# Masks added on VectorE from the fourth batch on, and a planner that knows that VectorE and GpSimd exclude each other

## The chip, the cores and the metric

One core of a Trainium2 chip runs the kernel. The metric is device time in microseconds (us). PE is TensorE, DVE is VectorE, ACT is ScalarE, POOL is GpSimd and SP is SyncE, whose queue issues nearly all transfers.

## What is computed

Attention over 8 batches, 8 heads, 576 positions and head size 64, followed by a gated two-layer network over all 4608 tokens (512 to 2048 to 512), all in float32:

```
scores = q k^T / 8, per batch and head
mask, heads 0-3 ("local"):   0 <= row - col < 32
mask, heads 4-7 ("strided"): row >= col and row % 32 == col % 32
attn = softmax(scores where the mask holds, else -1e9)
x    = (attn v), heads side by side, 4608 x 512
h    = x w_in ;  g = h * clip(h + 3, 0, 6) / 6 ;  out = g w_out
```

## The kernel before

**Network.** To keep float32 precision each large product is made of three passes over operands split into a high part and a remainder ("hi" and "lo"). Batches 0 to 2 go through the network one at a time (`ffn`, lines 921 to 923 for the first layer, 854 to 856 for the second). The other five, with the 64 rows left over of every batch, go in three pairs (`ffn_pair`), where one level of a Strassen-like scheme makes seven products of eight (lines 1094 to 1096). Before a pair starts, `combine_x` takes differences of its inputs (line 1039) and splits the results in hi (ACT, line 1030) and lo (POOL or DVE, line 1033). `split_g` splits the gated values in the same way (ACT line 887, POOL line 890). During the first batches the weights come in, are rebuilt and split (lines 311 to 337), and `combine_weights` makes the weight sums for the pairs (lines 974 to 995).

**Attention.** It runs between the network's products, two heads at a time, in `kept_pair`: 32 head pairs, of which 16 are local and 16 strided. For one head pair j = 0, 1:

1. PE, `scores`: two PSUM banks get the mask first, as a product of the identity `eye` with the mask (line 597: 96x384 for a local head, 128x144 for a strided one; line 601 masks one 32x32 corner of a local head more), and the small score products are accumulated on it (line 608, 72 of them for a local pair, 128 for a strided one).
2. `keep` copies each bank to the SBUF tile `e` (ACT line 619, or DVE line 621, whichever the planner finds earlier).
3. DVE takes row maxima (631), POOL subtracts them (653), ACT takes exp (656), DVE sums (659), adds 1e-9 from a tile `eps` and inverts (663, 664), POOL multiplies (668).
4. DVE transposes (708, 713), PE multiplies by v (402, 771), ACT or DVE put the result away.

Only steps 1 and 2 lose or gain instructions in this change, besides the added 1e-9 in step 3.

**What sets the order.** Nothing is dispatched when the kernel runs. A planner (`Plan`) gets every operation with the engines that can do it, an assumed duration on each, what it reads and writes and a due time. `emit` then plays the program through once: it takes again and again the engine and operation that can start first, and writes the instructions in that order. Each engine so has a fixed list, in which an instruction at the head that waits holds up all behind it. For some operations `emit` also chooses the engine. The assumed durations decide the order of the lists, never the duration of an instruction.

Of the kernel before, what the change touches and what calls it, by code (L numbers as in the profile page):

```python
# [10 lines left out]
F32 = mybir.dt.float32  # L11
F32R = mybir.dt.float32r
BF16 = mybir.dt.bfloat16
# [7 lines left out]
P = 128  # L21
# [18 lines left out]
HIENG = {"ACT": 0.63, "POOL": 1.2}  # L40
# [5 lines left out]
SOLO = 3  # L46
PAIRS = ((3, 4), (5, 6), (7, "l"))
# [15 lines left out]
PATIENCE = 2.0  # L63


class Plan:
# [12 lines left out]
    def op(self, engine, us, fn, reads=(), writes=(), due=0.0, room=0.0, mode="", after=0.0, take=None, give=None, early=0.0, words=6):  # L79
# [13 lines left out]
        self.ops.append((how, fn, before, due, room, mode, after, take, give, early, words))  # L93
        return n

    def emit(self, idle):
# [10 lines left out]
        mode, dma = "", 0.0  # L107
# [11 lines left out]
        while done < len(ops):  # L119
            done += 1  # L120
            best = None
            for e, r in ready.items():
                t0, first, kept = free[e], None, 0.0
                for due, n in sorted(r):
                    t = max(t0, avail[n] + (PATIENCE if e == "DVE" and avail[n] > WARM and len(ops[n][0]) > 1 else 0.0))
# [9 lines left out]
                if first is not None and (best is None or first[0] < best[0]):  # L135
                    best = (first[0], e, first[2])
            t, e, n = best
            how, fn, _, due, _, m, after, take, give, _, words = ops[n]
# [48 lines left out]
def attention_ffn(ctx: ExitStack, tc, q, k, v, w_in, w_out, out):  # L187
# [34 lines left out]
    eps = const.tile([P, 2, 8], F32, name="eps")  # L222
# [4 lines left out]
    mtri = const.tile([P, NPOS], BF16, name="mtri")  # L227
    left = [const.tile([P, B * LEFT], F32, name=f"left{c}") for c in range(NCC)]

    def identity():  # L230
        nc.vector.memset(three, 3.0)
        nc.vector.memset(eps, 1.0e-9)
# [30 lines left out]
    op("POOL", 2.2, masks, reads=[("ident",)], writes=["const"], due=-22)  # L263

# [25 lines left out]
    def weight_part(k, w, g, i):  # L290
# [52 lines left out]
        op("DVE", 0.95, join, reads=[key], writes=[fkey], due=due - 3)  # L343
        op(HIENG, 0, hi, reads=[fkey], writes=[key], due=due - 2)
        op({"POOL": 1.4, "DVE": 0.75}, 0, lo, reads=[fkey, key], writes=[key + ("lo",), key], due=due - 1)
# [94 lines left out]
    def kept_pair(g):  # L440
# [150 lines left out]
        sb = [slot(early) for _ in range(2)]  # L591

        def scores():
            ps = [psum(sb[j], f"ps{nm}{j}")[:n, :cols].rearrange("p (u x) -> p u x", x=w) for j in range(2)]
            m = (mband if loc else mtri).unsqueeze(1).to_broadcast([n, nblk, w])
            for j in range(2):
                nc.tensor.matmul(ps[j], eye[:n, :n], m, start=True, stop=False)
            if loc:
# [3 lines left out]
            for i in range(nblk):  # L602
                for a in range(n // PAD):
                    for j in range(2):
# [4 lines left out]
                                         qk_of("k")[own, k0:k0 + w], start=False, stop=i == nblk - 1)  # L609
# [4 lines left out]
        def keep(e, j):  # L614
# [3 lines left out]
            if e == "ACT":  # L618
# [669 lines left out]
```

## Time and profile before

| | us |
|---|---|
| median of three runs (lowest to highest) | 929.01 (928.42 to 932.99) |
| the profiled execution | 929.12 |
| its span, from first to last instruction | 927.3 |
| PE busy | 885.3 (95%) |
| DVE busy | 488.8 (53%) |
| POOL busy | 428.6 (46%) |
| ACT busy | 404.6 (44%) |

The execution that was profiled took 929.12 us, 1.8 us more than its span. In the rows of a timeline the first number is the start in us from the start of the span, the second the duration, and in brackets stands how long the engine was idle ahead of it and what ended that. In rows of a group the last two numbers before the second bar are the busy time in us and the mean duration of one in ns. Matmul instructions overlap in a pipeline: a product of 512 columns is shown as 0.39 us long, but the next one starts 0.23 us after it, and it is the distance of the starts that tells what a product costs.

### The profile page before, as it was taken

To read this page: it belongs to the slowest core of one execution; us is meant where nothing else is said; L and a number is where in the kernel's file an instruction comes from. 1 tells how busy PE (TensorE), PEld (TensorE's weight loads), DVE (VectorE), ACT (ScalarE), POOL (GpSimd) and SP (SyncE) were. 2 spreads that over 40 slices of the span, in tenths; PEclk is the share of its full clock that TensorE was granted. 3 is DMA by queue.
4 is the path that set the end of the run, shared out by engine and by line. 5 is a ranking of instruction groups with operands and counts; after the bars stand their busy time and mean duration, and the time that the engine had idled before them with its cause. 6 is when DMAs were issued, how large, how long until landed. Compare 5 with 4: busy or idle time off the path is not lost.

```text
span 927.3 us, 19470 instructions
## 1 busy us (share of the span) xinstructions
PE 885.3 (95%) x7747; PEld 711.9 (77%) x7747; DVE 488.8 (53%) x833; ACT 404.6 (44%) x736; POOL 428.6 (46%) x378
## 2 busy tenths in 40 slices
PE   5789898999999999999999999999999999999997
PEld 3668686776888788888788778888887887888786
DVE  3788866568766777466755723345457003323200
ACT  2656655333434435344444633444446234334421
POOL 3646765555765877222221955213139531112441
PEclk7579999999999999999999999999999999999999
DMA  9988999977688874799784687785745675555374
GB/s 161 236 251 206 249 236 333 282 177 190 181 197 242 209 189 112 205 260 230 218 209 149 194 257 196 238 210 192 227 156 211 200 236 185 194 192 188 120 213 137
DMA packets 229563, 191.71 MB, mean 207 GB/s; under 512 B 174944, under 2 KB 189280, under 8 KB 229472
## 3 DMA queue, kind: packets, MB, share of 16 engines
q1 hardware_dynamic: 226800, 189.35, 73.2%
q10 hardware_dynamic: 2672, 1.11, 0.6%
q8 instruction: 61, 1.00, 0.5%
q14 instruction: 30, 0.25, 0.1%
HBM read 157.91 MB, written 32.51 MB: 205 GB/s over the span
## 4 chain that ended last, share of the span: by engine, by line
PE 75%; POOL 6%; DMA 6%; DVE 5%; SPq 3%; issue 2%; ACT 2%; DVEq 0%; POOLq 0%; ACTq 0%
PE ph L1094 8%; PE ph L1095 7%; PE ph L1096 7%; PE acc L854 4%; PE acc L856 4%; PE acc L855 4%; PE ph L921 3%; PE ph L922 3%; PE ph L923 3%; PE ps L608 3%; DMA rawi<-in_moe_w_in_dram 3%; DMA qn<-in_q_dram 2%; POOL xc L1033 2%; PE acc2b L854 2%; PE acc2b L856 2%
## 5 line engine op out<-in xcount | busy, mean ns | idle before, releaser
L1113 DVE TENSOR_TENSOR htmp<-ph,htmp 128x512 f32<-128x512 f32 x72 | 49.7, 690 | 183.9 <-ACT htmp L1105 106.7
L1094 PE MATMUL ph<-xc,wi 128*128 128x512 f32 x336 | 133.4, 397 | 1.3 <-DVE htmp L1113 0.8
L1095 PE MATMUL ph<-xc,wi 128*128 128x512 f32 x336 | 131.1, 390 | 0.0
L1096 PE MATMUL ph<-xc,wi 128*128 128x512 f32 x336 | 130.9, 390 | 0.0
L890 POOL TENSOR_TENSOR g<-u,g 128x512 fp32r<-128x512 f32 x48 | 65.7, 1372 | 62.1 <-ACT g L887 50.1
L921 PE MATMUL ph<-x,wi 128*128 128x512 f32 x192 | 79.8, 415 | 7.9 <-DVE u L960 4.6
L922 PE MATMUL ph<-x,wi 128*128 128x512 f32 x192 | 76.8, 400 | 4.0 <-DVE x L433 2.6
L923 PE MATMUL ph<-x,wi 128*128 128x512 f32 x192 | 76.7, 399 | 0.8 <-POOL wi L337 0.8
L854 PE MATMUL acc<-wo,g 128*128 128x512 f32 x192 | 76.9, 401 | 0.0
L855 PE MATMUL acc<-wo,g 128*128 128x512 f32 x192 | 75.1, 391 | 1.5 <-issue 1.1
L1094 PEld LDWEIGHTS ph<-xc,wi 128*128 128x128 f32 x336 | 63.0, 188 | 17.2 <-DVE htmp L1113 2.0
L856 PE MATMUL acc<-wo,g 128*128 128x512 f32 x192 | 75.4, 392 | 0.2 <-POOL g L890 0.2
L1096 PEld LDWEIGHTS ph<-xc,wi 128*128 128x128 f32 x336 | 63.1, 188 | 13.4
L1095 PEld LDWEIGHTS ph<-xc,wi 128*128 128x128 f32 x336 | 63.1, 188 | 12.4
L708 DVE STREAM_TRANSPOSE atloc<-e 32x192 f32<-32x192 f32 x168 | 61.9, 369 | 15.9 <-POOL e L668 9.0
L1105 ACT COPY htmp<-ph 128x512 f32<-128x512 f32 x72 | 42.2, 587 | 50.0 <-PE ph L1096 48.1
L653 POOL TENSOR_TENSOR e<-e,st 128x288 f32<-128x288 f32 (+1 forms) x30 | 34.2, 1141 | 64.5 <-DVE st L631 64.4
L890 POOL TENSOR_TENSOR g12a<-u,g02a 128x512 fp32r<-128x512 f32 x16 | 20.6, 1289 | 83.4 <-ACT g02a L887 83.4
L956 ACT ACTIVATE u<-htmp,three 128x512 f32<-128x512 f32 x48 | 34.7, 723 | 44.5 <-DVE htmp L1113 44.5
L956 ACT ACTIVATE u<-ph,three 128x512 f32<-128x512 f32 x48 | 33.0, 688 | 44.2 <-PE ph L923 43.8
L960 DVE SCALAR_TENSOR_TENSOR u<-u,htmp 128x512 f32<-128x512 f32 x48 | 38.5, 802 | 22.9 <-ACT u L956 22.8
L890 POOL TENSOR_TENSOR g11a<-u,g01a 128x512 fp32r<-128x512 f32 x16 | 21.5, 1347 | 60.4 <-ACT g01a L887 52.2
(212 smaller groups left out, 2079.5 us busy)
## 6 DMA issues: line engine op xcount, KB each, us to landing
wo<-wod SPq DMA_DIRECT2D x128, 512.0 KB
wi<-wid SPq DMA_DIRECT2D x84, 512.0 KB
rawi<-in_moe_w_in_dram SPq DMA_DIRECT2D x16, 512.0 KB
rawo<-in_moe_w_out_dram SPq DMA_DIRECT2D x16, 512.0 KB
wod<-wo SPq DMA_DIRECT2D x16, 512.0 KB
wid<-st SPq DMA_DIRECT2D x64, 128.0 KB
qn<-in_q_dram SPq DMA_DIRECT2D x112, 72.0 KB
kn<-in_k_dram SPq DMA_DIRECT2D x112, 72.0 KB
```

Of the source, the lines that this page charges most:

```text
L708: nc.vector.transpose(at[PAD * (a + h):PAD * (a + h) + PAD, :, PAD * a:PAD * a + PAD], e[PAD * a:PAD * a + PAD, :, PAD * h:PAD * h + PAD])
L854: nc.tensor.matmul(acc, gh, woh, start=fc == 0, stop=False)
L855: nc.tensor.matmul(acc, gh, wol, start=False, stop=False)
L856: nc.tensor.matmul(acc, gl, woh, start=False, stop=end)
L890: on(e).tensor_tensor(out=to(1), in0=tiles[uk], in1=tiles[gk[0]].bitcast(F32), op=ALU.subtract)
L921: nc.tensor.matmul(ph, wih, xh, start=n_ == 0, stop=False)
L922: nc.tensor.matmul(ph, wih, xl, start=False, stop=False)
L923: nc.tensor.matmul(ph, wil, xh, start=False, stop=n_ == NCC - 1)
L956: nc.scalar.activation(make(), src(), AF.Relu, bias=three)
L1094: nc.tensor.matmul(ph, w[:, j, 0], x[:, 0], start=u in (0, 1, 3) and j == 0, stop=False, skip_group_check=u in (2, 4, 5, 6))
L1095: nc.tensor.matmul(ph, w[:, j, 0], x[:, 1], start=False, stop=False, skip_group_check=u in (2, 4, 5, 6))
L1096: nc.tensor.matmul(ph, w[:, j, 1], x[:, 0], start=False, stop=j == 1, skip_group_check=u in (2, 4, 5, 6))
```

## The change

It has two parts.

**The masks.** From batch 3 on (`ADDED = 3`), so for 20 of the 32 head pairs, the products of lines 597 and 601 are left out; each small score product now starts and ends its own piece of the bank (`start=added`). `keep` is then DVE's alone: one addition of the bank and a mask, 96x384 with the new tile `mwhole` for a local head, 128x144 with `mtri` for a strided one. POOL fills `mwhole` once (a copy of six masks and a memset).

**The planner.** An operation can be marked `port`. Marked ones on DVE and POOL are planned so that none overlaps another on the other engine. Marked are the operations of POOL in attention, the splits, sums and differences of weights and inputs, POOL's `split_g`, and a gate on DVE whose second input lies in SBUF. Some assumed durations are changed with it (POOL's high part of a weight from 1.2 to 0.62 us), the delay that kept DVE from taking shared work early is 0 for marked operations, and ties between engines are broken by due time. The 1e-9 is now added as a constant, so `eps` is gone.

Parts left out of the diff only mark further operations with `port=True` and change assumed durations by a few hundredths.

```
-HIENG = {"ACT": 0.63, "POOL": 1.2}
+HIENG = {"ACT": 0.63, "POOL": 0.62}
...
+ADDED = 3
...
-PATIENCE = 2.0
+PATIENCE = {("DVE", False): 2.0, ("DVE", True): 0.0, ("POOL", True): 0.0}
+PORT = ("DVE", "POOL")
...
-                    t = max(t0, avail[n] + (PATIENCE if e == "DVE" and avail[n] > WARM and len(ops[n][0]) > 1 else 0.0))
+                    t = max(t0, avail[n] + (PATIENCE.get((e, ops[n][11]), 0.0) if avail[n] > WARM and len(ops[n][0]) > 1 else 0.0))
+                    if ops[n][11] and e in PORT:
+                        t = max(t, port)
...
-                if first is not None and (best is None or first[0] < best[0]):
-                    best = (first[0], e, first[2])
+                if first is not None and (best is None or first[:2] < best[3]):
+                    best = (first[0], e, first[2], first[:2])
...
             free[e] = end = t + (us() if callable(us) else us)
+            if shared and e in PORT:
+                port = end - 0.13
...
+    def whole_mask():
+        nc.gpsimd.tensor_copy(mwhole, mband.unsqueeze(1).to_broadcast([QB, NQB, 2 * PAD]))
+        nc.gpsimd.memset(mwhole[:PAD, 0, :PAD], NEG)
+    op("POOL", 0.9, whole_mask, reads=["const"], writes=["mwhole"], due=T0 + TILE + 20, early=T0 + TILE)
...
-        op({"POOL": 1.4, "DVE": 0.75}, 0, lo, reads=[fkey, key], writes=[key + ("lo",), key], due=due - 1)
+        op({"POOL": 1.29, "DVE": 0.68}, 0, lo, reads=[fkey, key], writes=[key + ("lo",), key], due=due - 1, port=True)
...
+        added = b >= ADDED
...
-            for j in range(2):
+            for j in range(0 if added else 2):
                 nc.tensor.matmul(ps[j], eye[:n, :n], m, start=True, stop=False)
-            if loc:
+            if loc and not added:
...
-                                         qk_of("k")[own, k0:k0 + w], start=False, stop=i == nblk - 1)
+                                         qk_of("k")[own, k0:k0 + w], start=added, stop=added or i == nblk - 1)
...
-            if e == "ACT":
+            if added:
+                nc.vector.tensor_tensor(out=e_own(j), in0=ps, in1=mwhole if loc else mtri.unsqueeze(1).to_broadcast([n, nblk, w]), op=ALU.add)
+            elif e == "ACT":
                 nc.scalar.copy(e_own(j), in_halves(ps))
...
-            nc.vector.tensor_tensor(out=x, in0=x, in1=eps[:n, :, :nblk], op=ALU.add)
+            nc.vector.tensor_scalar_add(x, x, 1.0e-9)
...
-                op({"POOL": 0.74, "DVE": 0.42}, 0, mix, reads=w, writes=[w[to[0]]], due=due + kc + 0.1)
+                op({"POOL": 0.74, "DVE": 0.42}, 0, mix, reads=w, writes=[w[to[0]]], due=due + kc + 0.1, port=True)
```

**How the lists move.** Line numbers of the changed kernel are 10 to 13 higher behind the inserted lines: 608 becomes 619, 890 becomes 903, 1033 becomes 1046, 1039 becomes 1052. The first place is PE's list at the scores of a local head pair of the first pair of batches; `ps_10` and `ps_11` are its two banks. Before:

```order
L856 MATMUL acc0a_5177<-wo_5604,g10a_5880 128x512
L597 LDWEIGHTS eye
L597 MATMUL ps_10_5970<-mband,eye 96x384
L597 MATMUL ps_11_5971<-mband,eye 96x384
L601 LDWEIGHTS eye
L601 MATMUL ps_10_5970<-mfirst,eye 32x32
L601 MATMUL ps_11_5971<-mfirst,eye 32x32
L608 MATMUL ps_10_5970<-kplain,qplain 32x64
L608 MATMUL ps_11_5971<-kplain,qplain 32x64
```

After:

```order
L867 MATMUL acc0a_5170<-wo_5584,g00a_5823 128x512
L868 MATMUL acc0a_5170<-wo_5584,g00a_5823 128x512
L869 MATMUL acc0a_5170<-wo_5584,g10a_5832 128x512
L619 MATMUL ps_10_5957<-kplain,qplain 32x64
L619 MATMUL ps_11_5958<-kplain,qplain 32x64
```

The four mask products and their weight loads are gone; the network's product stands directly ahead of the first score product.

The second place is POOL's list where the second pair of batches is got ready (`combine_x`) while the first pair's products still run; `g10a` is the lo part of a gated value, which PE waits for, `xc` and `hxf` are the inputs that are split and subtracted. Before:

```order
L1033 TENSOR_TENSOR xc_3_6487<-hxf_2009,xc_3_6487 128x512
L890 TENSOR_TENSOR g10a_6520<-u_14_6460,g00a_6500 128x512
L1033 TENSOR_TENSOR xc_3_6512<-hxf_2062,xc_3_6512 128x512
L1033 TENSOR_TENSOR xc_6_6528<-hxf_2089,xc_6_6528 128x512
L1033 TENSOR_TENSOR xc_6_6545<-hxf_2099,xc_6_6545 128x512
L1039 TENSOR_TENSOR hxf_2089<-hxf_2089,hxf_2009 128x512
L1039 TENSOR_TENSOR hxf_2099<-hxf_2099,hxf_2062 128x512
L890 TENSOR_TENSOR g10a_6590<-u_15_6561,g00a_6573 128x512
L890 TENSOR_TENSOR g10b_6607<-g_0_5208,g00b_6582 128x512
```

After:

```order
L1052 TENSOR_TENSOR hxf_2055<-hxf_2088,hxf_2055 128x512
L1046 TENSOR_TENSOR xc_1_6404<-hxf_2098,xc_1_6404 128x512
L903 TENSOR_TENSOR g10a_6458<-u_14_6411,g00a_6451 128x512
L1052 TENSOR_TENSOR hxf_2068<-hxf_2098,hxf_2068 128x512
L1046 TENSOR_TENSOR xc_6_6476<-hxf_2088,xc_6_6476 128x512
L1052 TENSOR_TENSOR hxf_2088<-hxf_2088,hxf_2055 128x512
L1046 TENSOR_TENSOR xc_4_6463<-hxf_2068,xc_4_6463 128x512
L1052 TENSOR_TENSOR hxf_2088<-hxf_2088 128x512
L903 TENSOR_TENSOR g10a_6549<-u_15_6510,g00a_6539 128x512
L903 TENSOR_TENSOR g10b_6564<-g_0_5167,g00b_6529 128x512
```

From the first `xc` of this place on, eleven operations of lines 1033 and 1039 and two `g10a` stand ahead of the last `g10a` before, and nine of lines 1046 and 1052 and one `g10a` after. In all POOL has fourteen operations of these two lines at this place before and twelve after; the other two have gone to DVE. Over the whole program POOL's share of line 1033 goes from 27 to 19 and of line 1039 from 15 to 21, DVE's from 15 to 23 and from 9 to 3; of the weights' remainders (line 337) three go from DVE to POOL, and of their high parts (lines 327 and 329) four from ACT to POOL.

The third place is DVE's list at the strided scores that follow the local ones of the first place. Before:

```order
L960 SCALAR_TENSOR_TENSOR u_11_6266<-u_11_6266,htmp_1984 128x512
L631 TENSOR_REDUCE st_3_6273<-e 128x16
L659 TENSOR_REDUCE st_3_6273<-e 128x16
L663 TENSOR_TENSOR st_3_6273<-st_3_6273,eps 128x16
L664 RECIPROCAL st_3_6273<-st_3_6273 128x16
L1113 TENSOR_TENSOR htmp_1984<-ph_6_1_6288,htmp_1984 128x512
```

After:

```order
L1126 TENSOR_TENSOR htmp_1988<-ph_6_1_6166,htmp_1988 128x512
L973 SCALAR_TENSOR_TENSOR u_12_6191<-u_12_6191,htmp_1988 128x512
L630 TENSOR_TENSOR e<-ps_30_6193,mtri 128x8x18
L630 TENSOR_TENSOR e<-ps_31_6194,mtri 128x8x18
L644 TENSOR_REDUCE st_3_6263<-e 128x16
L672 TENSOR_REDUCE st_3_6263<-e 128x16
L676 TENSOR_SCALAR st_3_6263<-st_3_6263 128x16
L677 RECIPROCAL st_3_6263<-st_3_6263 128x16
```

The two evictions are new in DVE's list, directly ahead of the row maxima, which were there before.

More of the change, by code (lines that the diff above doesn't have):

```diff
@@ L77, in __init__, with op @@
         self.by = {}
-    def op(self, engine, us, fn, reads=(), writes=(), due=0.0, room=0.0, mode="", after=0.0, take=None, give=None, early=0.0, words=6):
+    def op(self, engine, us, fn, reads=(), writes=(), due=0.0, room=0.0, mode="", after=0.0, take=None, give=None, early=0.0, words=6, port=False):
         n = len(self.ops)
@@ L92, in op @@
         how = engine if isinstance(engine, dict) else {engine: us}
-        self.ops.append((how, fn, before, due, room, mode, after, take, give, early, words))
+        self.ops.append((how, fn, before, due, room, mode, after, take, give, early, words, port))
         return n
@@ L134, in emit @@
                         first = (t, due, n)
-                if first is not None and (best is None or first[0] < best[0]):
-                    best = (first[0], e, first[2])
-            t, e, n = best
-            how, fn, _, due, _, m, after, take, give, _, words = ops[n]
+                if first is not None and (best is None or first[:2] < best[3]):
+                    best = (first[0], e, first[2], first[:2])
+            t, e, n, _ = best
+            how, fn, _, due, _, m, after, take, give, _, words, shared = ops[n]
             for x in how:
@@ L227, in attention_ffn @@
     mtri = const.tile([P, NPOS], BF16, name="mtri")
+    mwhole = const.tile([QB, NQB, 2 * PAD], BF16, name="mwhole")
     left = [const.tile([P, B * LEFT], F32, name=f"left{c}") for c in range(NCC)]
@@ L678, in kept_pair @@
             op("DVE", red, most, reads=[ekey, ekey + "1"], writes=[stkey], due=sd + 0.7)
-            op("POOL", pool, less, reads=[stkey, ekey + "1"], writes=[ekey], due=sd + 1)
+            op("POOL", pool, less, reads=[stkey, ekey + "1"], writes=[ekey], due=sd + 1, port=True)
             op("ACT", 0.2 + 0.0017 * cols, exp, writes=[ekey], due=sd + 1.5)
@@ L961, in gate_of @@
         op("ACT", 0.69, relu, reads=reads, writes=[uk], due=due)
-        op({"DVE": 0.69, "POOL": 1.4} if both else {"DVE": 0.69}, 0, gate, reads=reads, writes=[uk], give=give, due=due)
+        op({"DVE": 0.69, "POOL": 1.4} if both else {"DVE": 0.69}, 0, gate, reads=reads, writes=[uk], give=give, due=due, port=give is not None)
     def combine_weights(g, due):
@@ L974, in whole @@
                     on(e).tensor_tensor(out=tiles[tk.key].rearrange("p (u x) -> p u x", u=FQ), in0=a, in1=d, op=ALU.add)
-                op({"POOL": 1.34, "DVE": 0.69}, 0, whole, reads=[key, key + ("lo",), "tmps"], writes=[tk], take=tk, due=due + kc, early=due)
+                op({"POOL": 1.3, "DVE": 0.69}, 0, whole, reads=[key, key + ("lo",), "tmps"], writes=[tk], take=tk, due=due + kc, early=due, port=True)
                 w.append(tk)
@@ L1002, in combine_weights @@
                 op("ACT", 0.63, hi, reads=[w[i]], writes=[sk, sk + ("lo",)], due=due + kc + 0.2)
-                op({"POOL": 1.34, "DVE": 0.69}, 0, lo, writes=[sk, w[i]], due=due + kc + 0.3, give=w[i])
+                op({"POOL": 1.3, "DVE": 0.69}, 0, lo, writes=[sk, w[i]], due=due + kc + 0.3, give=w[i], port=True)
                 op("SP", 1.4, put, reads=[sk], writes=[("wid", 7 * (2 * g + f) + u, kc) for f in range(2) for u in us], due=due + 3, after=2.0)
```

24 lines of the change are left out of this document (11 added, 13 removed).

## The prediction

> **What bounds the kernel now.** I read the page's head and its chain first, then the busy time by stretch, then single places of the timeline.
>
> ```profile
> span 927.3 us, 19470 instructions
> PE 885.3 (95%) x7747; PEld 711.9 (77%) x7747; DVE 488.8 (53%) x833; ACT 404.6 (44%) x736; POOL 428.6 (46%) x378
> PE 75%; POOL 6%; DMA 6%; DVE 5%; SPq 3%; issue 2%; ACT 2%; DVEq 0%; POOLq 0%; ACTq 0%
> ...
> 0.00:75.00 75.00, 56.06 (x908) 43.23 (x909) 49.32 (x97) 36.92 (x76) 39.39 (x63) 0.73 0.99 215
> 75.00:222.00 147.00, 136.96 (x1388) 107.74 (x1389) 108.01 (x189) 73.56 (x137) 88.67 (x74) 1.00 0.90 244
> 222.00:500.00 278.00, 277.24 (x3134) 223.20 (x3134) 188.81 (x344) 123.42 (x237) 138.73 (x121) 1.00 0.77 201
> 500.00:545.00 45.00, 42.80 (x212) 34.31 (x212) 26.14 (x26) 24.48 (x44) 32.15 (x22) 1.00 0.70 208
> 545.00:690.00 145.00, 145.00 (x1120) 118.43 (x1119) 60.67 (x109) 56.72 (x98) 41.44 (x34) 1.00 0.70 208
> 690.00:725.00 35.00, 32.70 (x140) 25.80 (x141) 18.59 (x16) 20.40 (x37) 32.47 (x23) 1.00 0.56 199
> ```
>
> The last six rows give, per stretch: its length, then busy us of PE, weight loads, DVE, ACT and POOL (instructions in brackets), the granted clock, the DMA share, GB/s. Up to 75 us PE lacks 18.9 us and the DMA share is 0.99: inputs and weights come in. From 75 to 222 it lacks another 10.0. From 222 to 500 and from 545 to 690 it lacks 0.8 us in 423, at full clock: there every product that goes is time that goes. In the two stretches where the next pair's inputs are got ready (500 to 545, 690 to 725) it lacks 2.2 and 2.3, and POOL is the fullest of the others (32.47 of 35.00). All 20 head pairs that the change touches have their scores between 222 and 679 us (the evictions in line 619's row below start from 224.1 to 678.5), nearly all in the full stretches.
>
> **The masks on PE.** One local and one strided pair, and a place where the network's products are followed at once by small ones with no mask between:
>
> ```profile
> 467.74 0.39 PE L856 MATMUL acc0a<-wo,g10a 128*128 128x512 f32 x1
> 467.97 0.49 PE L597 MATMUL ps<-mband,eye 96*96 96x384 bf16 x2
> 468.39 0.21 PE L601 MATMUL ps<-mfirst,eye 32*32 32x32 bf16 x2
> 468.53 0.97 PE L608 MATMUL ps<-kplain,qplain 64*32 64x64 f32 x72
> ...
> 489.83 0.39 PE L856 MATMUL acc0a<-wo,g10a 128*128 128x512 f32 x1
> 490.06 0.30 PE L597 MATMUL ps<-mtri,eye 128*128 128x144 bf16 x2
> 490.29 1.27 PE L608 MATMUL ps<-kplain,sq 64*32 64x18 f32 x128
> ...
> 485.66 0.39 PE L1096 MATMUL ph<-xc,wi 128*128 128x512 f32 x1
> 485.98 1.28 PE L402 MATMUL pv<-atloc,vloc 128*64 128x96 f32 x28
> ```
>
> By distances of starts: the local masks take 468.53 - 467.97 = 0.56 us, the strided ones 490.29 - 490.06 = 0.23. But the network's product ahead of them costs 0.23 (467.97 - 467.74), and ahead of small products without a mask it costs 0.32 (485.98 - 485.66). That change of kind, 0.09, now falls to it. So a local pair saves 0.56 - 0.09 = 0.47 and a strided one 0.23 - 0.09 = 0.14; ten of each make 4.7 + 1.4 = **6.1 us**. No row shows a network product directly ahead of line 608, so this is bounded: if the change of kind is free there, 5.6 + 2.3 = 7.9; if the first weight load (0.11 us by the row below), which now has no mask to hide under, shows as well, 20 x 0.11 less, 3.9. I take 6.1, since line 402 is the nearest case.
>
> **The evictions on DVE.** Forty copies leave ACT and forty additions come to DVE.
>
> ```profile
> L608 PEld LDWEIGHTS ps<-kplain,qplain 64*32 64x32 f32 x1152 | 13.9, 113 | 0.6
> L1113 DVE TENSOR_TENSOR htmp<-ph,htmp 128x512 f32<-128x512 f32 x72 | 49.7, 690 | 183.9 <-ACT htmp L1105 106.7
> L619 ACT COPY e<-ps x40: 263/381/482, 224.1 to 678.5; 96x384 f32<-96x384 f32 x20, 128x144 f32<-128x144 f32 x20
> L621 DVE COPY e<-ps x4: 307/426/554, 16.1 to 104.6; 96x384 f32<-96x384 f32 x2, 128x144 f32<-128x144 f32 x2
>   ACT e L619: 46.2, 14
> ```
>
> DVE's own copies of these banks took 0.307 us (144 columns) and 0.554 (384); an addition with one input in PSUM took 0.690 for 512 (line 1113), less than 0.554 x 512 / 384 = 0.739. So I price an addition like the copy of its size: 20 x 0.554 + 20 x 0.307 = 17.2 us of DVE; the copies are the lower end, 40 x 0.690 = 27.6 the upper one : 13.8 of the 17.2 for the 16 pairs in 222 to 500, where DVE has 89 us to spare. I cost them at nothing on the path. What hides them: PE has the network's products to go on with, and DVE stood idle 46.2 us (last row: idle time of DVE ahead of its rows on `e` between 222 and 690 that ACT's copy ended, 14 times) in which it waited for just these evictions; now it does them then. Behind an eviction in DVE's list stand the row maxima, which need it anyway, and only then the next gate. Without that cover the price is the 17.2 (a rival below). [...]
>
> **The planner's new order.** The pieces of work are the same but for a few that change engines, so what it can win are stalls of PE. The ones behind POOL and DVE in the two full-POOL stretches:
>
> ```profile
> 529.83 1.72 POOL L890 TENSOR_TENSOR g10a<-u,g00a 128x512 fp32r<-128x512 f32 x1
> 531.61 0.50 PE L856 MATMUL acc0a<-wo,g10a 128*128 128x512 f32 x1 [1.52 <-POOL g10a L890]
> 537.49 0.50 PE L854 MATMUL acc0b<-wo,g00b 128*128 128x512 f32 x1 [0.59 <-ACT htmp L866]
> 706.98 0.50 PE L1094 MATMUL ph<-xc,wi 128*128 128x512 f32 x1 [0.43 <-DVE g L960]
> 710.29 0.50 PE L856 MATMUL acc1a<-wo,g11a 128*128 128x512 f32 x1 [1.21 <-POOL g11a L890]
> 718.04 0.50 PE L856 MATMUL acc1b<-wo,g11b 128*128 128x512 f32 x1 [0.65 <-POOL g11b L890]
> ...
> 519.25 1.30 POOL L1033 TENSOR_TENSOR xc<-hxf,xc 128x512 fp32r<-128x512 f32 x1
> 517.25 0.68 DVE L1039 TENSOR_TENSOR hxf<-hxf 128x512 f32<-128x512 f32 x1
> 533.27 1.78 DVE L1033 TENSOR_TENSOR xc<-hxf,xc 128x512 fp32r<-128x512 f32 x1
> ```
>
> At 531.61 PE waits 1.52 us for the last `g10a`. Ahead of it, counted from the first `xc`, stood 13 operations in POOL's list; now there are 10. Three fewer at 1.30 each are 3.9 us, more than the wait: **1.5 us** saved, at most 2.2 (all that PE lacks in that stretch). Around 710 the `g11a` in question is the fourteenth from the first `xc` both before and after: nothing. A DVE operation with two SBUF inputs takes 0.68 us alone and 1.78 beside POOL, so each operation that POOL gives up adds one to DVE that POOL in turn may have to wait for; with two of them at 0.68 the gain is still 3.9 - 1.4 = 2.5, over 1.52. [...]
>
> Before 222 us the list changes on every engine: `kp` ahead of `qp`, and of the weights three remainders and four high parts come to POOL.
>
> ```profile
> 12.55 1.19 PE L498 MATMUL qp<-ident,qn 72*128 72x72 f32 x8 [2.47 <-DMA qn<-in_q_dram]
> L337 POOL TENSOR_TENSOR wi<-fi,wi 128x512 fp32r<-128x512 f32 x12 | 17.0, 1419 | 0.5 <-ACT wi L327 0.2
> L329 POOL CAST wo<-fo 128x512 fp32r<-128x512 f32 x9 | 6.3, 700 | 12.8 <-DVE fo L319 11.3 <-ACT left L419 1.5
> PE ph L921 <- DVE u L960: 4.6, 4, 2.2
> PE ph L923 <- POOL wi L337: 0.8, 1, 0.8
> PE acc L855 <- POOL wo L337: 0.5, 1, 0.5
> ```
>
> For the better, the four waits for DVE's gate (4.6 us in all) could go, as DVE has less to do there; for the worse, POOL gets 3 x 1.42 + 4 x 0.70 = 7.1 us more, and PE already waits for its remainders at two places (last two rows). If `kn` lands ahead of `qn`, whose landing PE awaited 2.47 us, the first scores start up to that much sooner; its landing isn't shown. I take 0 between -4.6 and +7.1, since SP's list is the same for its first 62 rows and the DMA share of 0.99 sets the pace up to 75 us. The added 1e-9 and the `mwhole` copy are off the path: DVE and POOL have 39 and 58 us free between 75 and 222.
>
> **The sum.** 929.12 - 6.1 - 1.5 = **921.5 us**, made against the profiled execution, which is within 0.11 of the median 929.01. [...]
>
> **Rivals.**
>
> *The start gives it back.* POOL becomes what PE waits for while weights are split, between 75 and 222. For it: POOL gets more there, and PE waited for its remainders already. Against it: the two waits were 1.3 us together, and POOL was busy 88.67 of 147. If all 7.1 us landed on PE: 921.5 + 7.1 = 928.6, no change.
>
> *DVE's list becomes the bound.* An eviction at the head of DVE's list waits for its scores, and gates and sums that release PE's banks wait behind it. For it: DVE was the fullest engine beside PE in 222 to 500 (188.81 of 278), and PE did wait for its gate four times earlier on. Against it: it waited there for nothing of note from 222 to 500. With every eviction on the path: 921.5 + 17.2 = 938.7. It decides from the point where more than 7.6 of the 17.2 show, some 18 of 40 evictions: from there the kernel is slower than before.
>
> *The order wins more.* Half of the 10.0 us that PE lacks between 75 and 222, and the 1.9 of line 890 around 710 go as well: 921.5 - 5.0 - 1.9 = 914.6. For it: the old plan let DVE and POOL run side by side where the trace shows 1.78 for 0.68. Against it: the list around 710 has its `g11a` at the same place.
>
> **Chances.** Forecast 0.60 (its own range 917.5 to 925.0, from the bounds 3.9 and 7.9 of the masks and about 2 of order), start gives it back 0.17, DVE 0.11, more 0.12. A measurement of this kernel can tell about 0.5% from no change, 4.6 us: faster is below 924.4. The forecast lies there for 0.51 of its 0.60, "more" wholly: faster 0.63. The rest of the forecast and 0.16 of the first rival make same 0.25. Slower 0.12 is DVE and what the start could cost beyond 7.1. The range 914.5 to 931.0 leaves out about half of "more" (0.05) and the slower cases (0.12).
>
> **What would show it.** The masks: the first score product 0.32 us behind the network's product ahead of it, and each pair's stage on PE shorter by 0.47 or 0.14. The evictions: 0.31 and 0.55 us each, row maxima no later behind the scores than now, and no new wait of PE for DVE from 222 on. The order: no wait for `g10a` around 525. It would be wrong if PE lacks more than 10 us between 75 and 222, or more than 1 us between 222 and 500.

## The result, and the profile after

The changed kernel takes **922.57 us** (median of 8 runs, 918.54 to 925.55) where the kernel before, on the same chip, takes 929.56 (927.68 to 933.06): ratio **0.9915, 95% interval 0.9889 to 0.9941**. Ratios here are worked out over all undisturbed runs and not from the two medians, and one disturbed run of a kernel below (the masks alone), of 1254.29 us, is left out of its ratio. The changed kernel is faster by more than the 0.5% that can be told from no change, and lies 1.1 us from the forecast. The profiled execution took 918.60 us, so it is one of the shortest; the trace tells where a run of 918.6 us has its time. The page's head, its chain, and the busy time in the same six stretches as shown of before (length, then PE, weight loads, DVE, ACT, POOL, then clock, DMA share, GB/s):

```profile
span 916.8 us, 19372 instructions
PE 880.2 (96%) x7686; PEld 709.1 (77%) x7686; DVE 510.0 (56%) x886; ACT 387.9 (42%) x681; POOL 429.2 (47%) x381
PE 78%; DVE 5%; DMA 3%; SPq 2%; issue 2%; POOL 2%; ACT 1%; DVEq 0%; ACTq 0%; POOLq 0%
...
0.00:75.00 75.00, 57.71 (x918) 44.44 (x919) 51.78 (x104) 39.55 (x77) 45.80 (x70) 0.73 0.93 213
75.00:222.00 147.00, 140.20 (x1460) 110.65 (x1459) 108.50 (x191) 68.83 (x125) 89.16 (x80) 0.98 0.90 247
222.00:500.00 278.00, 273.37 (x3023) 220.27 (x3022) 199.28 (x376) 112.72 (x205) 136.40 (x115) 1.00 0.78 203
500.00:545.00 45.00, 44.27 (x219) 35.65 (x219) 29.98 (x32) 25.52 (x44) 28.96 (x20) 1.00 0.73 225
545.00:690.00 145.00, 144.96 (x1112) 118.54 (x1112) 67.47 (x121) 58.45 (x99) 50.32 (x39) 1.00 0.67 198
690.00:725.00 35.00, 35.00 (x155) 28.53 (x154) 15.73 (x13) 16.20 (x29) 26.95 (x19) 1.00 0.75 259
```

POOL's share of the chain fell from 6% to 2%. PE is busy 5.1 us less in all (885.3 to 880.2). What it lacks by stretch, length less busy time: up to 75 us 18.9 before and 17.3 now; 75 to 222, 10.0 and 6.8; **222 to 500, 0.8 and 4.6**; 500 to 545, 2.2 and 0.7; 690 to 725, 2.3 and 0.0. So the forecast's number was met with one loss in it that was not forecast, and more gain elsewhere.

**A measure that the start blurs less.** Runs of one kernel differ by 3 to 10 us here, and two profiles of the changed kernel show the first network product at 42.25 and 41.27 us, and the end of the first pass over the network at 170.83 and 171.33. I therefore also read the *tail*: from the start of the last product of that first pass (the last `acc` of tile 0) to the start of the last product of all (`acc2b`). Those two rows of the timeline, before:

```profile
172.36 0.39 PE L856 MATMUL acc<-wo,g 128*128 128x512 f32 x1
...
922.24 0.39 PE L856 MATMUL acc2b<-wo,ge 128*128 128x512 f32 x1
```

and of the changed kernel, with one row more between them that is used below:

```profile
170.83 0.39 PE L869 MATMUL acc<-wo,g 128*128 128x512 f32 x1
...
219.16 0.39 PE L869 MATMUL acc<-wo,g 128*128 128x512 f32 x1
...
911.75 0.39 PE L869 MATMUL acc2b<-wo,ge 128*128 128x512 f32 x1
```

The tail fell from 749.9 to 740.9 us, by 9.0. The same kernel profiled again below has 741.2, and a kernel whose order differs from before's only at the start has 749.7 against 749.9.

These pairs agree within 0.3 us, but a tail of one profile isn't always that good. The row at 219.16 is the 264th `acc` product, the last one ahead of batch 3's first scores. Up to it the changed kernel and seven of the kernels below have the same instructions on PE, DVE, ACT and POOL, and from the first row to this one their nine traces take from 47.2 to 51.4 us. The two longest (49.5 and 51.4) hold a stretch in which PE ran at half its clock (granted clock 0.50). Kernels with this start are therefore also compared *behind 220*, from the start of the 264th `acc` product to the start of the last `acc2b`: 692.6 us for the changed kernel, 693.4 when it was profiled again. All 20 pairs whose masks moved lie in both measures. Before's order has less other work ahead of its 264th product, so against it only the tail is used.

### The profile page after: what moved, and what is told of

Its sections match the earlier page's. It is cut to its first block, busy times and chain, and to the rows that moved or that the text cites. A ratio compares the mean times of both kernels' runs of the same rounds, so it can differ in the third digit from the quotient of the medians.

```text
span 916.8 us, 19372 instructions
## 1 busy us (share of the span) xinstructions
PE 880.2 (96%) x7686; PEld 709.1 (77%) x7686; DVE 510.0 (56%) x886; ACT 387.9 (42%) x681; POOL 429.2 (47%) x381
## 4 chain that ended last, share of the span: by engine, by line
PE 78%; DVE 5%; DMA 3%; SPq 2%; issue 2%; POOL 2%; ACT 1%; DVEq 0%; ACTq 0%; POOLq 0%
PE ph L1107 9%; PE ph L1109 8%; PE ph L1108 8%; PE acc L867 4%; PE ph L934 3%; PE acc L868 3%; PE acc L869 3%; PE ph L936 3%; PE ph L935 3%; PE ps L619 3%; PE pv L412 2%; PE acc1a L867 2%; PE acc2b L867 2%; PE acc1b L867 2%; PE acc1a L869 2%
## 5 line engine op out<-in xcount | busy, mean ns | idle before, releaser
L903 POOL TENSOR_TENSOR g<-u,g 128x512 fp32r<-128x512 f32 x48 | 63.5, 1326 | 61.0 <-ACT g L900 41.1
L1109 PEld LDWEIGHTS ph<-xc,wi 128*128 128x128 f32 x336 | 63.1, 188 | 13.8 <-issue 0.5
L1108 PEld LDWEIGHTS ph<-xc,wi 128*128 128x128 f32 x336 | 63.1, 188 | 12.3
L681 POOL TENSOR_TENSOR e<-e,st 128x288 f32<-128x288 f32 (+1 forms) x30 | 35.6, 1186 | 33.9 <-DVE st L677 29.9
L666 POOL TENSOR_TENSOR e<-e,st 128x288 f32<-128x288 f32 (+1 forms) x30 | 34.2, 1140 | 35.6 <-DVE st L644 31.4
L903 POOL TENSOR_TENSOR g10a<-u,g00a 128x512 fp32r<-128x512 f32 x16 | 20.6, 1289 | 64.0 <-ACT g00a L900 52.4
```

The costliest lines, as they stand in the source:

```text
L903: on(e).tensor_tensor(out=to(1), in0=tiles[uk], in1=tiles[gk[0]].bitcast(F32), op=ALU.subtract)
L1108: nc.tensor.matmul(ph, w[:, j, 0], x[:, 1], start=False, stop=False, skip_group_check=u in (2, 4, 5, 6))
L1109: nc.tensor.matmul(ph, w[:, j, 1], x[:, 0], start=False, stop=j == 1, skip_group_check=u in (2, 4, 5, 6))
```

## The experiments

All are compared with the kernel before on the same chip. Four kernels part the change first.

**The order alone.** Every mask stays on TensorE; the planner's new prices, waits and shared port are kept.

```diff
-ADDED = 3
+ADDED = 99
```

> The new order alone: the planner's new prices, waits and shared port as in the changed kernel, every mask still added by TensorE and the scores evicted as before the change. Theory (three parts that add up: masks -6.1 us on TensorE, evictions in VectorE's list +3.5, order -4.4, together the -7.0 that was measured): 925.2 us, with the waits of PE for g10a, g11a and g11b gone. [...] Rival B (the order did it all, the masks only move PE's work): 922.6.

Measured: 922.18 us, ratio 0.9913 (0.9888 to 0.9937): by itself as much as the whole change, as rival B's 922.6 had it, and 3.0 us less than my theory. The tail is 745.4, 4.5 under before. PE lacks 2.5 us in 222 to 500, 0.2 in 500 to 545 and 0.1 in 690 to 725. That the order only moves stalls, and leaves this run at the time of before, is refuted; of the 1.5 us that I gave the order, the trace shows three times as much. On rival B the traces and the runs differ: behind 220 the trace has 697.0 us here, 3.6 to 4.4 more than those of the changed kernel, with a stretch at half clock in it (0.50 from 366.4 to 369.7 us), and it was taken in one of the longer runs (925.42 of 918.56 to 928.00).

**The masks alone.** The planner of before, with its prices; masks of batches 3 and later added by VectorE (the planner orders anew, as it now knows those evictions). Cut, against the kernel before:

```diff
+ADDED = 3
...
+        added = b >= ADDED
...
-            for j in range(2):
+            for j in range(0 if added else 2):
...
-            if e == "ACT":
+            if added:
+                nc.vector.tensor_tensor(out=e_own(j), in0=ps, in1=..., op=ALU.add)
+            elif e == "ACT":
```

> The masks alone: the planner of before with its prices, and from the fourth batch on the masks added by VectorE as it evicts. Theory: -6.1 for the masks and +3.5 for evictions that stand ahead of gates in VectorE's list, 927.0 us, with new waits of PE for DVE's u between 222 and 340. [...] Rival B: 929.6. If instead the new order is what makes the waits for u (not the evictions), it is 923.5 without such waits.

Measured: 929.53 us, ratio 0.9981 (0.9972 to 0.9990), 1.8 us less than before; tail 749.3, 0.6 less. The row of 222 to 500 and its longest waits of PE (total, times, longest):

```profile
222.00:500.00 278.00, 271.55 (x3077) 216.96 (x3076) 204.88 (x372) 111.30 (x204) 142.36 (x121) 1.00 0.77 200
PE ph L1105 <- issue: 1.9, 1, 1.9
PE ps L617 <- DVE x L441: 1.4, 1, 1.4
PE pv L410 <- DVE e L628: 1.3, 1, 1.3
```

PE lacks 6.5 us there where it lacked 0.8: what the masks free, waits of several kinds take back. The expected waits for `u` between 222 and 340 are not among them, so the place that I named was wrong; the last row shown is a wait for an eviction (`e`, line 628).

**Masks on both engines, in the changed kernel's order.** The mask products go back to TensorE beside VectorE's addition (the masks are added twice). **Masks on TensorE, the 40 evictions on ScalarE, in the same order.** The second differs from the first only in who evicts:

```diff
-            for j in range(0 if added else 2):
+            for j in range(2):
...
-            if loc and not added:
+            if loc:
```

and in the second also:

```diff
-            if added:
-                nc.vector.tensor_tensor(out=e_own(j), in0=ps, in1=..., op=ALU.add)
-            elif e == "ACT":
+            if added or e == "ACT":
                 nc.scalar.copy(e_own(j), in_halves(ps))
```

> The changed kernel in its own order, with the mask products put back on TensorE beside VectorE's addition (the masks are added twice). Against the changed kernel this is the price of the mask products alone. Theory: 20 pairs at 0.47 or 0.14 us, +6.1, so 928.7 us (926.5 to 930.5 by the bounds 3.9 and 7.9); the first score product again 0.56 or 0.23 behind the network's product plus its 0.23. [...] Rival B (PE has slack where the masks stood, since it then waits for the gate anyway): less than +2, at most 924.6.

> The changed kernel's own order of everything else, with the masks on TensorE and the same 40 evictions made by ScalarE at the places where VectorE made them. Against the run with the masks added twice this is the price of the 40 evictions on VectorE. Theory (evictions ahead of gates cost 3.5 us between 222 and 340): 928.7 - 3.5 = 925.2 us, and the waits for u there are gone. Rival A (evictions wholly hidden): 928.7, the same as with the masks twice. A third way (ScalarE's list holds them up, as it was idle time of DVE behind ACT's evictions before: 46.2 us): above 930.

Measured: 924.79 us, 0.9931 (0.9913 to 0.9948), tail 745.4; and 925.77, 0.9938 (0.9923 to 0.9952), tail 746.3. So at a fixed order the evictions on VectorE are hardly dearer than those on ScalarE: the ratios agree within their intervals, and behind 220 the traces have 697.5 us with them and 696.8 without. (The tail is 0.9 us shorter with them, but the other trace has a stretch at half clock, 0.50 at 203 to 207 us, ahead of the first moved mask.) Against the changed kernel the mask products alone cost 4.0 to 4.9 us behind 220 and 1.5 to 1.9 by the ratios: less than the theory's 6.1, and by the ratios what rival B had, under 2. My theory that the evictions cost 3.5 us fell here, although 925.77 is near the 925.2 that it gave; by the waits, PE waits for `u` 1.8 to 1.9 us in 222 to 500 in both runs.

The next three leave the masks out altogether, or look at the start.

**Keys first.** Before's planner with the new rule for ties alone.

```diff
-                if first is not None and (best is None or first[0] < best[0]):
+                if first is not None and (best is None or first[:2] < best[3]):
```

> The kernel before with one line of the planner changed: of two operations on different engines that could start at the same time, the one that is due sooner is put down first. The only thing this moves is kp ahead of qp at the start (the two transposes of the first pair, and their copies); everything behind stands as before. Theory S (the new order's gain comes in good part from the start, whose first network product stood 2.9 us earlier with the order alone): 3 us less than before, ratio 0.997. Rival J (it is lost again before the end of the first pass over the network, as that end stood 0.8 us later there in spite of the earlier start, so the gain of the order comes from the joints): within 0.5 us of before, ratio 1.000.

Measured: 929.10 us, ratio 0.9983 (0.9965 to 1.0002); first network product at 44.88 instead of 45.59, tail 749.7. That is 1.6 us by the runs and not told from nothing; the rule is at most a part of what the start gives.

**No masks, in before's order** and **in the changed kernel's order**, both with the evictions on ScalarE. Cut: the corner masks and the start flags follow in both, and in the second ScalarE evicts as above.

```diff
+            left_out = b >= 3
-            for j in range(2):
+            for j in range(0 if left_out else 2):
```

> The kernel before in its own order, with the mask products of the fourth and later batches left out and nothing put in their place (the masks are missing there, the evictions stay on ScalarE). Theory M (the mask products cost PE 6.1 us, and what ate them in the run with the masks alone was the evictions in VectorE's list): 6.1 us less than before, ratio 0.9934. Rival W (a PE that is ahead runs into the gates and sums of the other engines in 222 to 500, whoever evicts): about 1.8 us less, ratio 0.998, and PE lacks about 6 us in 222 to 500 instead of 0.8.

> The changed kernel's order with the 40 evictions on ScalarE and the mask products of the fourth and later batches left out, nothing in their place (the masks are missing there). Against the run with these masks on TensorE and these evictions on ScalarE (ratio 0.9938) it gives the masks' price in the new order: theory M 6.1 us less, ratio 0.987; rival W 2 us less, ratio 0.9915. Against the changed kernel (ratio 0.9915) it gives the price of VectorE's evictions: nothing if they are hidden in the new order (the two runs before this one differed by 0.9 us), 4 us if the evictions take the gain.

Measured in before's order: 923.90 us, ratio 0.9924 (0.9897 to 0.9950), tail 744.8: 5.0 us shorter, where theory M had 6.1. PE stays full:

```profile
222.00:500.00 278.00, 277.12 (x3132) 222.84 (x3120) 189.82 (x346) 125.38 (x241) 139.70 (x121) 1.00 0.78 204
```

Rival W, that a PE which is ahead must wait for the others whoever evicts, is refuted by this row: without the new evictions, in the order that suits the old ones, it lacks 0.9.

In the changed kernel's order: 919.25 us, ratio 0.9878 (0.9852 to 0.9903). The two rows of the tail and the 264th `acc` product between them, with the masks on TensorE (evictions on ScalarE):

```profile
172.03 0.39 PE L867 MATMUL acc<-wo,g 128*128 128x512 f32 x1
...
221.54 0.39 PE L867 MATMUL acc<-wo,g 128*128 128x512 f32 x1
...
918.30 0.39 PE L867 MATMUL acc2b<-wo,ge 128*128 128x512 f32 x1
```

and without them:

```profile
170.08 0.39 PE L868 MATMUL acc<-wo,g 128*128 128x512 f32 x1
...
217.39 0.39 PE L868 MATMUL acc<-wo,g 128*128 128x512 f32 x1
...
911.61 0.39 PE L868 MATMUL acc2b<-wo,ge 128*128 128x512 f32 x1
```

The tails are 746.3 and 741.5, but 2.2 of these 4.8 us lie ahead of the first moved mask. Behind 220, at 696.8 and 694.2, the masks are worth 2.6 us in the traces, and 5.6 by the ratios (0.9938 less 0.9878). The waits of PE in 222 to 500 of the run without masks and without VectorE's evictions:

```profile
PE ph L933 <- DVE u L972: 2.3, 3, 0.9
PE ps L620 <- issue: 1.1, 1, 1.1
```

and of the changed kernel, which has them:

```profile
PE ph L934 <- DVE u L973: 2.3, 3, 0.9
PE ps L619 <- issue: 1.0, 1, 1.0
PE pv L412 <- DVE e L630: 0.9, 1, 0.9
```

The waits for the gate's `u` are the same to a tenth with VectorE's evictions and without. They belong to the order. The last row, 0.9 us for an eviction (`e`, line 630), is not among the waits without them. One of the waits for `u`, with what DVE does meanwhile, in the changed kernel's timelines of PE and of DVE:

```profile
243.93 0.50 PE L934 MATMUL ph<-x,wi 128*128 128x512 f32 x1 [0.74 <-DVE u L973]
...
239.58 3.58 DVE L726 STREAM_TRANSPOSE at<-e 32x256 f32<-32x256 f32 x8
243.19 0.69 DVE L973 SCALAR_TENSOR_TENSOR u<-u,ph 128x512 f32<-128x512 f32 x1
243.79 1.01 DVE L630 TENSOR_TENSOR e<-ps,mwhole 96x384 f32<-96x384 f32 x2
```

The gate stands behind eight transposes of the strided softmax, 3.58 us, and the evictions come after it.

**The changed kernel again.** 

> The changed kernel itself once more, beside the two runs without masks on the same chip. Its runs so far lay between 918.5 and 925.6, those of the order alone between 918.6 and 928.0, so 8 runs each can't tell whether the masks bring 0 or 4 us on top of the order. Theory M with hidden evictions: 4 to 6 us below the order alone, ratio 0.987. Rival W: the same as the order alone, ratio 0.9913.

Measured: 923.46 us, ratio 0.9911 (0.9885 to 0.9937), tail 741.2. By the ratio that is rival W's number (0.9913), not theory M's 0.987. Against the run without masks (tail 741.5, behind 220 694.2) VectorE's evictions cost nothing in the traces (741.2 and 693.4); by the ratios they cost 0.0033, 3 us. The two kernels have the same instructions in the same order up to 219 us, so their starts differ by chance alone. Both profiled runs of the changed kernel (918.60 and 919.35) lie at the low end of its own 14 runs (918.5 to 925.6), so what its other runs lose more is in no trace here, and this difference stays open.

The last four try the limits.

**Each addition made twice.**

```diff
+                for _ in range(2):
                     nc.vector.tensor_tensor(out=e_own(j), in0=ps, in1=..., op=ALU.add)
```

> The changed kernel in its own order, with each of the 40 evictions that add a mask made twice on VectorE, one behind the other, into the same tile (the second only repeats the first): 20 x 0.545 + 20 x 0.299 = 16.9 us more of VectorE. If the evictions are hidden, as the prediction had it and as the traces from the end of the first network pass (about 171 us) on say (741.5 us without them, 740.9 and 741.2 with them): not over 1 us longer from there on, time within 2 us of the changed kernel, ratio 0.991 to 0.993. If they take the 3 to 4 us by which the medians stand apart (919.3 without, 922.6 and 923.5 with): 3 to 4 us more again, ratio 0.995. If wholly on the path: 16.9 more, ratio 1.009.

Measured: 926.29 us, ratio 0.9968 (0.9947 to 0.9989), tail 746.2. Of the second 16.9 us of VectorE 5.2 show in the tail, 5.6 to 6.4 behind 220, and 5 by the ratios. That is nearest to the second case, whose 0.995 lies inside the interval, but in the traces the first 16.9 us cost nothing: there the price of evictions is not one rate, and the cover seems nearly used up by the first.

**No shared port.** The order alone, without the rule that marked operations on DVE and POOL don't overlap.

```diff
-ADDED = 3
+ADDED = 99
...
-PORT = ("DVE", "POOL")
+PORT = ()
```

> The order alone (masks on TensorE, ratio 0.9913), with one rule of the planner taken out: operations that read two SBUF tiles on VectorE and GpSimd may again be planned side by side. The other planner edits stay. Theory: this rule is what took away the waits for g10a, g11a and g11b at the joints, 3.4 us; without it PE lacks 2 us or more again in each of the two joints and the ratio is 0.995. Rival: the high parts given to GpSimd and the smaller patience did it; the joints stay without waits, ratio 0.991. [...]

Measured: 945.30 us, ratio 1.0191 (1.0165 to 1.0218), tail 763.3, 17.9 longer than with the rule. Three stretches:

```profile
222.00:500.00 278.00, 268.05 (x3081) 213.32 (x3064) 195.03 (x347) 116.96 (x228) 125.62 (x101) 1.00 0.74 194
500.00:545.00 45.00, 42.95 (x212) 34.32 (x212) 30.88 (x39) 23.42 (x43) 25.44 (x18) 1.00 0.51 170
690.00:725.00 35.00, 32.07 (x165) 25.43 (x164) 27.17 (x35) 20.06 (x34) 23.14 (x17) 1.00 0.47 166
```

Both joints lack 2 us or more again (2.1 and 2.9), as expected, though PE now waits for ACT's `htmp` at both (2.0 and 1.8 us), for `g11a` (1.2) at the second, and not for `g10a`. The largest part of the loss is in 222 to 500, where PE lacks 10.0 us instead of 2.5, which I hadn't expected. The planner's new prices (0.69 and 1.29 us) are near what such operations took with none of the other engine beside them (before, 0.68 us on DVE at 517.25 and 1.29 on POOL at 518.01); without the rule, as I read it, the planner believes them where they don't hold. In the traces 51 of VectorE's `TENSOR_TENSOR` and `SCALAR_TENSOR_TENSOR` operations take over 1.2 us here, 39 with the rule, 37 before. So the rule brings no fewer such operations than the dearer prices of before did; it seems to make the lower prices usable. That the rule alone would make the gain was not tried.

**From batch 5 on**, and **local pairs only**.

```diff
-ADDED = 3
+ADDED = 5
```

and for the other:

```diff
-        added = b >= ADDED
+        added = b >= ADDED and loc
```

> The changed kernel with the masks moved to VectorE only from the batch numbered 5 on (numbered from 0; the change has 3): the eight head pairs of batches 3 and 4 keep their masks on TensorE, and the planner orders anew. Theory: 8 of the 20 pairs' masks, 2.0 us of TensorE by what the runs gave per pair, come back; if the waits of PE for DVE's gate between 222 and 340 (2.3 us) come from VectorE's evictions they go, and the two cancel: ratio 0.991. If those waits come from the order alone, as the run without VectorE's evictions had them too, they stay where this order has them, and it is 2 us slower: ratio 0.993.

> The changed kernel with only the local pairs' masks moved to VectorE; the ten strided pairs keep masks on TensorE and may be evicted by either engine, and the planner orders anew. Theory (a strided pair saves 0.14 us, a local one 0.47): 1.4 us of TensorE come back, and VectorE has 6 us less to do; within 1.5 us of the changed kernel, ratio 0.991 to 0.9925. Rival (the evictions cost on the path what the medians say, 3 to 4 us for all, so over 1 us for the 20 strided ones): no loss or a gain, ratio 0.990.

Measured: 919.06 us, ratio 0.9891 (0.9873 to 0.9910), tail 743.6; and 920.22, ratio 0.9905 (0.9887 to 0.9923), tail 740.0. From batch 5 on, PE is full again in 222 to 500 (its row below, without waits for `u`), but lacks 1.5 us in 545 to 690:

```profile
222.00:500.00 278.00, 277.40 (x3123) 223.90 (x3123) 201.10 (x367) 118.63 (x222) 138.95 (x115) 1.00 0.80 205
```

Its tail is 2.5 us longer than the changed kernel's, but this lies ahead of the first moved mask, in instructions that both have: from the end of the first pass to the 264th `acc` product it took 51.4 us against 48.3 and 47.7, with half clock from 185.2 to 188.5 us (granted clock 0.50). Behind 220 it has 692.2 us against 692.6 and 693.4, and by the ratios it is 2 us faster. So the eight pairs' masks, put back on TensorE with an order of their own, cost nothing that shows. It was profiled once, in the longest of its runs (921.34 of 916.18 to 921.34). Both versions' intervals overlap the changed kernel's, so neither is shown to beat it. That the ten strided pairs' masks on VectorE are worth anything isn't seen: without them, in an order of its own, the tail is 0.9 us shorter, and the time behind 220, 692.4 us, is 0.2 to 1.0 shorter.

The runs together, with the end of the first pass, the tail, and for kernels of the changed kernel's start the time behind 220, read at the same rows in each trace:

| kernel | ratio to before | first pass ends | tail | behind 220 |
|---|---|---|---|---|
| before | 1 | 172.4 | 749.9 | - |
| masks alone | 0.9981 | 174.3 | 749.3 | - |
| keys first | 0.9983 | 171.2 | 749.7 | - |
| no masks, before's order | 0.9924 | 171.9 | 744.8 | - |
| order alone | 0.9913 | 173.2 | 745.4 | 697.0 |
| masks on TensorE, ScalarE evicts | 0.9938 | 172.0 | 746.3 | 696.8 |
| masks on both | 0.9931 | 172.2 | 745.4 | 697.5 |
| no masks, ScalarE evicts | 0.9878 | 170.1 | 741.5 | 694.2 |
| changed | 0.9915, 0.9911 | 170.8, 171.3 | 740.9, 741.2 | 692.6, 693.4 |
| additions twice | 0.9968 | 173.7 | 746.2 | 699.0 |
| no shared port | 1.0191 | 172.6 | 763.3 | - |
| from batch 5 | 0.9891 | 170.7 | 743.6 | 692.2 |
| local only | 0.9905 | 173.8 | 740.0 | 692.4 |

## Why the prediction was right, and where it was not

One step at a time in the changed kernel's order, the traces give: the order -3.6 us (tail 749.9 to 746.3; -5.8 without the 2.2 us that this trace takes more ahead of the first moved mask), the masks off PE -2.6 (696.8 to 694.2 behind 220), the evictions to VectorE -0.8 to -1.6 (to 693.4 and 692.6). The ratios give -5.8 (0.9938), -5.6 (to 0.9878) and +3 (to 0.9911 and 0.9915). Forecast: -1.5, -6.1 and 0. By both, the order brought much more than forecast and the masks, with their evictions, less: the sum held because two terms were off in opposite senses, and that it came within 1.1 us is luck. How much the masks and the evictions each took stays open, since traces and ratios differ; together they took 3.4 to 4.2 us by the traces and 2.1 to 2.5 by the ratios, and nothing by the ratio of the order alone (0.9913).

**The masks on PE: right in the rows, a little large in effect.** One strided and one local pair of the changed kernel:

```profile
448.76 0.40 PE L1109 MATMUL ph<-xc,wi 128*128 128x512 f32 x1
449.08 0.60 PE L619 MATMUL ps<-kplain,sq 64*32 64x18 f32 x49
...
468.60 0.39 PE L869 MATMUL acc0a<-wo,g10a 128*128 128x512 f32 x1
468.92 0.49 PE L619 MATMUL ps<-kplain,qplain 64*32 64x64 f32 x29
```

The first score stands 0.32 us behind the network's product in both, where before it stood 0.79 and 0.46 behind; so the 0.47 and 0.14 are exact, and the borrowed price of line 402 was the right one. The 6.1 came down to 4.0 to 4.9 us for masks on both against changed and to 2.6 for ScalarE's evictions with and without masks (both behind 220), and to 5.0 for before with and without (tails). At the new order PE lacks 1.0 to 1.7 us more in 222 to 500 once the masks are gone (3.6 to 4.6, and 2.7 to 4.4), among it 1.0 us in the middle of one strided pair's scores that no engine accounts for ("issue" in the rows above). The step that failed is "there every product that goes is time that goes": it holds for before's stretches, and the change itself made the largest of them less full.

**The evictions: priced right, and hidden in the trace.** The additions by operation (count, least, median and most ns, first and last start), and what DVE was idle for ahead of them:

```profile
L630 DVE TENSOR_TENSOR e<-ps,mwhole x20: 532/545/555, 221.3 to 632.6; 96x384 f32<-96x384 f32 x20
L630 DVE TENSOR_TENSOR e<-ps,mtri x20: 298/299/311, 234.2 to 674.0; 128x144 f32<-128x144 f32 x20
  PE ps L619: 27.6, 12
```

Together 16.9 us against my 17.2; the 46.2 us that DVE idled for ACT's evictions are gone, and it now idles 27.6 for the scores themselves. Two fixed-order pairs put the effect behind 220 at +0.7 us (masks on TensorE) and at -0.8 to -1.6 (without); by the ratios they are -0.7 and +3, so it isn't shown that they are hidden in every run. My test for this step, "more than 1 us between 222 and 500", came out against it at 4.6, and was a bad test: the kernel without a single such eviction lacks 4.4 there. "No new wait of PE for DVE from 222 on" came out against it too: 2.3 us for `u`, which the order brought, and 0.9 for an eviction. The cover seems to end close by, since a second 16.9 us cost 5.2 in the tail. With the old planner the masks alone kept only 1.8 of the 7.1 us that leaving them out saves, so the gain isn't there in every order; whether there it is the evictions or the order made for them that costs, no run parts.

**The order: the term that was mis-sized.** At the first joint the forecast was met: the wait for the last `g10a` is gone and the stretch lacks 1.5 us less. "Around 710 nothing" was wrong: the 1.21 and 0.65 us for `g11a` and `g11b` went too, and the stretch lacks 2.3 less. I had counted that `g11a` is the fourteenth operation from the first `xc` in both lists, and it is; but not when the first `xc` starts. POOL's timeline before, first `xc` and last `g11a`:

```profile
689.54 1.29 POOL L1033 TENSOR_TENSOR xc<-hxf,xc 128x512 fp32r<-128x512 f32 x1 [6.69 <-ACT xc L1030]
...
708.53 1.71 POOL L890 TENSOR_TENSOR g11a<-u,g01a 128x512 fp32r<-128x512 f32 x1
```

and now:

```profile
680.12 1.30 POOL L1046 TENSOR_TENSOR xc<-hxf,xc 128x512 fp32r<-128x512 f32 x1 [0.64 <-PE acc1a L869]
...
699.67 1.74 POOL L903 TENSOR_TENSOR g11a<-u,g01a 128x512 fp32r<-128x512 f32 x1
```

Before, POOL stood 6.69 us idle for ACT ahead of the joint; now 0.64. The last `g11a` ends at 701.4, 4.5 us ahead of the last `acc1a` product at 705.9; before it ended at 710.2 and PE was already waiting. Against this the order puts gates behind transposes between 222 and 340, which I had not priced and which is most of the 2.7 us that PE lacks there even with the masks on TensorE. And "before 222 us: 0, between -4.6 and +7.1": PE lacks 3.2 us less in 75 to 222 and 1.6 less ahead of it, but a product at half clock counts as busy for longer (0.63 us at 140.19, 0.40 at 145.71, rows below), and the end of the first pass moved by 1.5 us only (172.4 to 170.8). In the nine traces with the changed kernel's start it lies between 170.1 and 173.8, in three of before's order between 171.2 and 172.4. So a gain at the start is not shown, and the 0 stands.

**The rivals.** *The start gives it back*: no, the first pass doesn't end later than the scatter of these traces, though POOL got its extra work. *DVE's list becomes the bound*: no; it begins to at twice the additions. *The order wins more* (914.6) had the right mechanism for line 890 around 710; its gain between 75 and 222 is not shown, and it missed the 3.9 us lost in 222 to 500. *The order saves nothing*: the sum without its 1.5 us is 929.12 - 6.1 = 923.0, and the measured 922.57 is nearer to this number than to 921.5, so the time doesn't decide. What the rows show of the two engines is that operations took longer side by side: before, those of DVE with two SBUF inputs 0.68 us at 517.25, with POOL idle, and 1.78 at 533.27, beside POOL; POOL's `hxf` 1.29 at 518.01 and 1.74 at 515.04, beside DVE's. That VectorE and GpSimd exclude each other, as the title has it, is a reading that no run tested. That the order only moves the stall isn't borne out: the order alone gave 0.9913, with 39 of DVE's operations over 1.2 us against 37. As many operations are that long, and PE waits for fewer of them at the joints.

## What to carry to other kernels

Part a change that comes with a new order by running the order alone and the edit at a fixed order: here the order by itself gave the whole gain that the runs measured, and the edit under the old planner about a fifth of that. To see whether an engine will be waited for, count from when its list can start, not only how many operations stand ahead. Where runs scatter more than the effect, compare the stretch between two fixed instructions of the profile, begin it right ahead of the first instruction that the edit touches, and look at the granted clock in it: one trace is one run.

## What the runs showed of the hardware that was not expected

From 60 us on PE ran at half speed (granted clock 0.50) for 3.3 to 6.8 us around or behind some of its waits: before, from 63.1 to 69.9 us, around one of 2.63 that ended at 63.90; in the changed kernel from 63.8 to 67.2, behind one of 2.22 that ended at 62.56, and from 138.9 to 145.7, around one of 1.74 for a weight's remainder that ended at 139.59. The last of these in the timeline, and the busy times there, with the granted clock third from the end:

```profile
139.59 0.80 PE L936 MATMUL ph<-x,wi 128*128 128x512 f32 x1 [1.74 <-DVE wi L347]
140.19 0.63 PE L934 MATMUL ph<-x,wi 128*128 128x512 f32 x1
140.61 0.63 PE L935 MATMUL ph<-x,wi 128*128 128x512 f32 x1
...
145.31 0.57 PE L867 MATMUL acc<-wo,g 128*128 128x512 f32 x1
145.71 0.40 PE L868 MATMUL acc<-wo,g 128*128 128x512 f32 x1
145.95 0.40 PE L869 MATMUL acc<-wo,g 128*128 128x512 f32 x1
...
140.00:146.00 6.00, 6.00 (x16) 4.62 (x16) 5.19 (x13) 0.91 (x2) 2.45 (x3) 0.53 1.03 418
```

From 140.19 us on the products stand 0.42 to 0.43 apart, up to 145.31 (0.40 to the next, then 0.24): 13 products at 0.2 us too much, 2.6 us, more than the wait itself. It doesn't follow every wait: the masks alone had one of 2.60 us that ended at 64.45 us, and a granted clock of 1.00 from 64.5 to 75; keys first had one of 2.90 us that ended at 108.79, and 0.50 from 109.2 to 112.6. Between 60 and 240 us the three profiles of before's order show one such stretch each, those of the new order two or three, which would be 1 to 3 us each that the new order pays, by an estimate from the 2.6 here. In the same instructions it stands in some traces and not in others, at 185 and at 203 us for instance, and these two traces are the longest of the nine there; that it is what scatters the start was not tested. Ahead of the stretch at 139 us stood waits of 0.40, 0.74 and 1.74 us, with products between them; what switches the clock no run tested.

An addition of a bank in PSUM and one tile in SBUF kept its time beside POOL: 532 to 555 ns in 20 cases, 12 of them with an operation of POOL at the same time, where operations with two SBUF inputs on the same engine went from 0.68 to 1.78 us (before, at 517.25 and 533.27).
